# Retention two units to a burst, their kv in the banks of hp, beside a two-layer feed-forward on one Trainium2 core

## The chip, the cores and the metric

The kernel runs on one core of a Trainium2 chip. The metric is the device time of one execution in microseconds. Three runs of the kernel before took 873.88, 873.92 and 877.14 us; their median is 873.92 us.

## The reference

Linear attention with decay (retention), then two feed-forward layers without residuals:

```python
for t in range(S):                       # q, k, v: (4, 8, 768, 64)
    state = gamma[None, :, None, None] * state + np.einsum('bhd,bhe->bhde', k[:, :, t], v[:, :, t])
    y[:, :, t] = scale * np.einsum('bhd,bhde->bhe', q[:, :, t], state)
x = y.transpose(0, 2, 1, 3).reshape(3072, 512)
h = x @ w_in1                            # 512 x 2048
x = np.where(h > 0, h, np.exp(np.minimum(h, 0)) - 1) @ w_out1     # 2048 x 512
h = x @ w_in2                            # 512 x 1024
e = np.exp(h - h.max(-1, keepdims=True))
solu = h * e / (e.sum(-1, keepdims=True) + 1e-9)
ln = (solu - solu.mean(-1, keepdims=True)) / np.sqrt(solu.var(-1, keepdims=True) + 1e-6) * g_ln
out = ln @ w_out2                        # 1024 x 512
```

## The kernel before

**Precision.** Each product of the two layers is made of three matmuls on a high and a low part of both operands (`mm3`, lines 70 to 72), so that one product of 128x128 by 128x512 is three large matmuls.

**Retention in units.** A unit is 64 positions of one batch row with all eight heads; there are 48 (NU), in blocks of 8 (UPB). Four batch rows take turns, so the state that unit u leaves is used by unit u + 4. Per unit, TensorE makes scores (line 199), kv, the product of k and v that goes into the next state (line 206), and the values: state times q (line 246) and masked scores times v (line 249), all as 64x64 matmuls in a quarter of the array. The trace counts 16 instructions for the scores, 16 for kv, 16 for state times q and 16 for scores times v. VectorE reads the results from the two PSUM banks of the tile `ab`: `pt`, the masked scores (line 210), the output into `xf` (line 254) and the new state (line 223); ScalarE copies half of the state to the other partitions (line 226); GpSimd multiplies the state by its decay (line 233) and k by its factors (line 190); SP loads a unit's 576 KB (line 185) into one of three buffers.

**First layer in steps.** A block of 512 tokens (xf, split by `split_xh` on ScalarE and `split_xl` on VectorE into a high and a low part) goes through 16 steps, one for each 128 of the 2048 hidden columns; there are 6 blocks and 96 steps. Step s = 16 tb + k does `ff1_in(s)`, 12 large matmuls into `hp`, one of two PSUM banks (pool psh); the activation (`elu_a`: exp on ScalarE, line 304; `elu_b`: VectorE, lines 313 and 314, the last read of hp, then the cast gh on ScalarE, line 315, and gl on GpSimd, line 323); and `ff1_out(s - 2)`, 12 large matmuls into the four banks of `acc`. With the two of `ab` the eight PSUM banks are taken. At a block's last step the four banks of acc are copied out and stored.

**The order is written by hand.** Every engine takes its instructions in program order. The first block's retention runs ahead of step 0. From then on a unit's retention stands in a burst between `ff1_in(s)` and `ff1_out(s - 2)` of every odd step from 1 to 77, and of step 14: scores and kv of unit u + 1, then the values of unit u. The state of one burst is read in the next, so each engine has two steps for its part. At the last step of a block (k = 15) the next block's x is split: in the first block ahead of the activation, in the next four behind exp, with `elu_b` between the two splits. The split overwrites the x that `ff1_in` of that step reads, so it starts when these matmuls are over; `ff1_in` of the next step reads it.

**Second layer in 24 tiles** of 128 tokens. For tile i: `ff2_in(i)` (24 large matmuls into two banks), `norm_a(i)` (maximum, exp, product and sum; then the centering of z on GpSimd, line 394), `turn` and `turned` (a 32x32 transpose on VectorE, line 414, a store to DRAM and four loads back), `split_zh` on ScalarE and `split_zl` on VectorE, `norm_b`, and `ff2_out(i)` two tiles later (24 large matmuls, first reader of zh and zl). `split_y(i + 2)` casts the input of a later tile (line 366), when its load has landed.

Of the kernel before, what the change touches and what calls it, by code (L numbers as in the profile page):

```python
# [9 lines left out]
F32 = mybir.dt.float32  # L10
# [5 lines left out]
AF = mybir.ActivationFunctionType  # L16
ALU = mybir.AluOpType
# [4 lines left out]
P = 128  # L22
B, H, S, D = 4, 8, 768, 64
# [4 lines left out]
C = 64  # L28
NCH = S // C
# [6 lines left out]
NU = B * NCH  # L36
UPB = TB // C
LAG = 2
HL = NF1 - 1
SG = 2  # L40
HALF_N = 232
# [3 lines left out]
def tile_retention_ffn(ctx, tc, qkv, w_in1, w_out1, w_in2, w_out2, g_ln, dmask, odec, kgdec, ident_in, out):  # L45
# [28 lines left out]
    with tc.manual_schedule():  # L74
# [105 lines left out]
        blk = lambda t, p, base, n: t[half(p), base + n * D:base + (n + 1) * D]  # L180

        def load_unit(u):
            pool, n = (first_p, 4) if u < 4 or u == UPB - 1 else (at_p, 3)
            t = pool.tile([P, 18 * D], F32, tag="in", name="in", bufs=n)
            nc.sync.dma_start(out=t, in_=qkv[u])
            in_t[u] = t
# [5 lines left out]
        chunk = lambda u: u // UPB * (UPB // B) + u % UPB // B  # L192
        place = lambda u: u % B * (UPB // B) + u % UPB // B

        def att_scores(u, banks):
            t = in_t[u]
            for j, a, m in heads(lambda x, y, z: (y, z, x)):
                n = 2 * (a != j) + m
                nc.tensor.matmul(banks[j][half(a), m * C:(m + 1) * C], blk(t, j, K, n), blk(t, j, Q, n), start=True, stop=True)  # L199

        def att_kv(u, banks):
            t = in_t[u]
            if chunk(u) < NCH - 1:
                for j, a, m in heads(lambda x, y, z: (z, y, x)):
                    n = 2 * (a != j) + m
                    nc.tensor.matmul(banks[a][half(j), 4 * C + m * D:4 * C + (m + 1) * D], blk(t, a, KR, n), blk(t, a, V, n), start=True, stop=True)  # L206

        def att_mask(u, v):
            pt = at_p.tile([P, 2, 2 * C], F32, tag="pt", name="pt")
# [22 lines left out]
                four = lambda t: t.rearrange("p a (m d) -> p (a m) d", m=2)  # L232
                nc.gpsimd.tensor_tensor(four(sg_t[u]), four(s_t[u][0]), kg_sb[:, 1].unsqueeze(2).to_broadcast([P, 4, D]), ALU.mult)

        def att_values(u, banks):
            c = chunk(u)
            t, pt = in_t.pop(u), p_t.pop(u)
            col = lambda o: slice(2 * C + o * C, 2 * C + (o + 1) * C)
# [12 lines left out]
        def att_done(u, v):  # L251
            ci = place(u)
            four = lambda t: t.rearrange("p (a o) t -> p a o t", a=2)
            nc.vector.tensor_tensor(four(xf[:, :, ci * C:(ci + 1) * C]), v[:, :, 2 * C:4 * C].rearrange("p a (o t) -> p a o t", o=2), four(od_sb), ALU.mult)

        x_t = {}

# [121 lines left out]
        def norm_a(i):  # L379
            hp = h2.pop(i)  # L380
            st = sm_p.tile([P, 8], F32, tag="st", name="st")
            if i == 0:
                e, z = xf[:, :2], xf[:, 2:]
            else:
                e = z_p.tile([P, 2, 512], F32, tag="e2", name="e2")
                z = z_p.tile([P, 2, 512], F32, tag="z", name="z")
            nc.vector.tensor_reduce(st[:, 0:1], hp, AX.XY, ALU.max, negate=True)
            nc.scalar.activation(e, hp, AF.Exp, bias=st[:, 0:1], accum_out=st[:, 1:2])
            nc.vector.tensor_scalar(st[:, 2:3], st[:, 1:2], 1e-9, None, ALU.add)
            nc.vector.reciprocal(st[:, 3:4], st[:, 2:3])  # L390
            nc.vector.scalar_tensor_tensor(z, hp, st[:, 3:4], e, ALU.mult, ALU.mult, accum_out=st[:, 4:5])
            nc.vector.tensor_scalar(st[:, 5:6], st[:, 4:5], -1.0 / FF2, None, ALU.mult)  # L392
            if i < N2 - 1:
                nc.gpsimd.tensor_scalar(z, z, st[:, 5:6], 1.0, ALU.add, ALU.mult)  # L394
            else:
                t = z_p.tile([P, NF2, 4, 32], F32, tag="t", name="t")
                nc.gpsimd.tensor_scalar(t.rearrange("p c a f -> p a c f"), z.rearrange("p n (a c f) -> p (n a) c f", a=2, c=NF2), st[:, 5:6], 1.0, ALU.add, ALU.mult)
                z = t.rearrange("p c a f -> p (c a f)")
            zc_t[i] = (z, e if i else spare(), st)
# [119 lines left out]


        NS = NB * NF1
        for s in range(NS + LAG):
            tb, k = divmod(s, NF1)
            u = UPB + s // 2 + (s > NF1 - 2) if s % 2 else (2 * UPB - 1 if s == NF1 - 2 else NU)
            if s < NS:
                ff1_in(s)
                if k == NF1 - 1 and tb == 0:
                    split_xh(1, range(KD))
                    split_xl(1, range(KD))
                elu_a(s, tb == 0)  # L530
                if k == NF1 - 1 and 0 < tb < NB - 1:
                    split_xh(tb + 1, range(KD))
                    elu_b(s, tb == 0)
                    split_xl(tb + 1, range(KD))
            if u < NU:
                if u + 1 < NU:
# [3 lines left out]
                if u + 1 < NU:  # L540
                    att_mask(u + 1, both[1])
                att_done(u, both[1])
                if u + 1 < NU:
                    att_state(u + 1, both[1])
                if u + 2 < NU:
                    att_decay(u + 2)
                if u + 3 < NU:
                    load_unit(u + 3)
                if u + 2 < NU:
                    scale_k(u + 2)  # L550
            if tb == 0:
                prep_w(order1, slot)
                slot += 1
            if s < NS and (k < NF1 - 1 or tb in (0, NB - 1)):
                elu_b(s, tb == 0)
            if s == NS + LAG - 2:
                ff2_in(0)
                norm_a(0)
                turn(0)
                turned(0)  # L560
                norm_b(0)
                split_y(2)
            if s >= LAG:
                ff1_out(s - LAG)
            if tb == 0:
                prep_w(order1, slot)
                slot += 1
                elu_c(s, nc.vector)
            if s == HL:
                for i in range(slot, len(order1) + 2):  # L570
                    prep_w(order1, i)
                slot = len(order1) + 2
                ph0.close()
                ph0 = ExitStack()
                yt_p = ph0.enter_context(tc.tile_pool(name="yt0", bufs=3, side="right", reuse_waits="tile"))
            if u == NU - 1:
                ph0.close()
                right.close()
                pha.close()
                right = ExitStack()  # L580
                psr = right.enter_context(tc.tile_pool(name="psr", bufs=1, space=PSUM, side="right", reuse_waits="tile"))
                stage_p = right.enter_context(tc.tile_pool(name="stage2", bufs=5, side="right", reuse_waits="tile"))
                yi_p = right.enter_context(tc.tile_pool(name="yi", bufs=3, side="right", reuse_waits="tile"))
                yt_p = right.enter_context(tc.tile_pool(name="yt", bufs=3, side="right", reuse_waits="tile"))
                ys_p = right.enter_context(tc.tile_pool(name="ys", bufs=2, side="right", reuse_waits="tile"))
                new_top()
                nc.sync.dma_start(out=ident, in_=ident_in)
                nc.sync.dma_start(out=g_sb, in_=g_ln)
                for i in range(-4, 0):
                    prep_w(order2, i)  # L590
            if tb == NB - 1:
                prep_w(order2, k)
                if k in (1, 2, 3):
                    load_y(k - 1)
                if k in (9, 11):
                    split_y((k - 9) // 2)
            if tb == NB:
                prep_w(order2, NF1 + k)
# [4 lines left out]
        for i in range(1, N2):  # L603
# [4 lines left out]
            split_zh(i - 1)  # L608
            if i == 1:
                split_zl(0)  # L610
            if i + 2 < N2:
                split_y(i + 2)
            if i < N2 - 1:
                turn(i)
                turned(i)
            if i > 1:
# [79 lines left out]
```

## Time and profile before

| | |
|---|---|
| median of three runs | 873.92 us |
| the profiled execution | 874.49 us |
| its span, first to last instruction | 872.70 us |
| TensorE busy | 857.3 us (98%) |
| VectorE / ScalarE / GpSimd busy | 438.7 / 330.6 / 322.8 us |

The profile is of one execution. Its views have one row for an instruction or for a group of like ones: line of the kernel, engine, operation, output and inputs by name, shape; times in microseconds from the start of the span, durations in us or, where marked so, in ns. PE is TensorE, DVE VectorE, ACT ScalarE, POOL GpSimd, SPq the queue that issues the transfers. In the timeline a matmul's duration includes its way through the array, so the distance between two starts, not the duration, is what a matmul costs. In the chain the pieces follow each other from end to end.

### The profile page before, as it was taken

The numbers are of one execution on the slowest core, as the hardware profiler recorded it, in microseconds if no ns is written. First come the engines' busy times: TensorE is split into PE (matmuls) and PEld (weight loads), VectorE is DVE, ScalarE is ACT, GpSimd is POOL, SyncE is SP. The second block draws the span as 40 slices with busy tenths as digits, with TensorE's granted clock in tenths as the row PEclk, the third lists the DMA queues.
The fourth block names the chain that finished last, engine by engine and source line by source line (L and its number), as shares of the span: only waits on it lengthen the run. The fifth ranks groups of instructions, "written<-read, shape, count | busy, mean of one in ns | idle before, by whom it ended". The sixth has DMA issues, their size and how long they took to land.

```text
span 872.7 us, 15630 instructions
## 1 busy us (share of the span) xinstructions
PE 857.3 (98%) x6432; PEld 702.8 (81%) x6432; DVE 438.7 (50%) x736; ACT 330.6 (38%) x575; POOL 322.8 (37%) x321
## 2 busy tenths in 40 slices
PE   6899999999999999999999999999999999999998
PEld 5788888888888888888888878888788888888887
DVE  4899983222522233222422268796555555555552
ACT  3677762222322233222321245443343333333333
POOL 4555533322323232332322245553443333333330
PEclk9999999999999999999999999999999999999999
DMA  8677623111311113110311116310644444444432
GB/s 331 229 232 236 206 98 104 56 46 37 103 56 55 36 48 104 56 55 29 102 56 31 55 67 205 97 48 1 200 150 145 145 146 145 145 145 145 145 122 71
DMA packets 59735, 97.81 MB, mean 112 GB/s; under 512 B 4880, under 2 KB 41360, under 8 KB 59664
## 3 DMA queue, kind: packets, MB, share of 16 engines
q1 hardware_dynamic: 59664, 96.82, 34.0%
q8 instruction: 50, 0.82, 0.4%
q14 instruction: 21, 0.17, 0.1%
HBM read 72.16 MB, written 24.64 MB: 111 GB/s over the span
## 4 chain that ended last, share of the span: by engine, by line
PE 91%; DMA 3%; DVE 3%; ACT 1%; issue 1%; SPq 0%; POOL 0%; ACTq 0%; DVEq 0%
PE hp L71 14%; PE hp L72 14%; PE hp L70 14%; PE acc L70 11%; PE acc L72 10%; PE acc L71 10%; PE op L72 4%; PE op L70 4%; PE op L71 4%; PE ab L199 2%; DMA in<-in_qkv 2%; PE ab L206 1%; PE ab L246 1%; PE ab L249 1%; DMA zt<-t_dr 1%; DMA t_dr<-t 1%
## 5 line engine op out<-in xcount | busy, mean ns | idle before, releaser
L323 POOL TENSOR_TENSOR gl<-e,gh 128x512 fp32r<-128x512 f32 x80 | 106.9, 1336 | 310.9 <-issue 158.1
L70 PE MATMUL acc<-gh,w1oh 128*128 128x512 f32 x384 | 153.9, 401 | 0.4 <-ACT w1oh L138 0.4
L72 PE MATMUL acc<-gh,w1ol 128*128 128x512 f32 x384 | 150.0, 391 | 0.2 <-DVE w1ol L146 0.2
L71 PE MATMUL acc<-gl,w1oh 128*128 128x512 f32 x384 | 149.8, 390 | 0.0
L71 PE MATMUL hp<-xl,w1ih 128*128 128x512 f32 x380 | 147.9, 389 | 0.4 <-DVE xl L267 0.4
L70 PE MATMUL hp<-xh,w1ih 128*128 128x512 f32 x380 | 147.9, 389 | 0.0
L72 PE MATMUL hp<-xh,w1il 128*128 128x512 f32 x380 | 147.8, 389 | 0.0
L304 ACT ACTIVATE e<-hp 128x512 f32<-128x512 f32 x80 | 47.8, 597 | 186.0 <-PE hp L72 186.0
L313 DVE TENSOR_SCALAR e<-e 128x512 f32<-128x512 f32 x80 | 38.5, 481 | 136.3 <-ACT e L304 136.1
L315 ACT CAST gh<-e 128x512 fp32r<-128x512 f32 x96 | 59.6, 621 | 95.1 <-DVE e L314 82.7
L70 PEld LDWEIGHTS acc<-gh,w1oh 128*128 128x128 f32 x384 | 72.0, 188 | 17.1 <-ACT w1oh L138 0.8
L72 PEld LDWEIGHTS acc<-gh,w1ol 128*128 128x128 f32 x384 | 72.1, 188 | 15.9 <-DVE w1ol L146 0.6
L210 DVE TENSOR_TENSOR pt<-ab,dm_sb 128x256 f32<-128x256 f32 x43 | 18.1, 421 | 131.1 <-PE ab L249 124.6
L71 PEld LDWEIGHTS hp<-xl,w1ih 128*128 128x128 f32 x380 | 71.3, 188 | 15.7 <-DVE xl L267 0.9
L71 PEld LDWEIGHTS acc<-gl,w1oh 128*128 128x128 f32 x384 | 72.1, 188 | 14.0
L72 PEld LDWEIGHTS hp<-xh,w1il 128*128 128x128 f32 x380 | 71.3, 188 | 14.8
L70 PEld LDWEIGHTS hp<-xh,w1ih 128*128 128x128 f32 x380 | 71.3, 188 | 14.8
L117 POOL MEMSET raw<- 128x512 uint16 x48 | 61.0, 1279 | 48.7 <-DVE w1il L146 18.2
L394 POOL TENSOR_SCALAR z<-z,st 128x1024 f32<-128x1024 f32 x22 | 27.8, 1263 | 138.2 <-DVE st L392 138.2
L72 PE MATMUL op<-w2oh,zl 128*128 128x512 f32 (+1 forms) x192 | 74.2, 386 | 1.4 <-DVE zl L435 1.4
L70 PE MATMUL hp<-w2ih,yh 128*128 128x512 f32 x192 | 74.7, 389 | 0.0
L71 PE MATMUL hp<-w2il,yh 128*128 128x512 f32 x192 | 74.7, 389 | 0.0
(118 smaller groups left out, 1411.7 us busy)
## 6 DMA issues: line engine op xcount, KB each, us to landing
in<-in_qkv SPq DMA_DIRECT2D x48, 576.0 KB, 4.2
raw<-in_w_in SPq DMA_DIRECT2D x24, 512.0 KB, 3.8
raw<-in_w_out SPq DMA_DIRECT2D x24, 512.0 KB, 4.1
t_dr<-t SPq DMA_DIRECT2D x22, 512.0 KB, 2.8
zt<-t_dr SPq DMA_DIRECT2D x88, 128.0 KB, 2.5
y_dr<-yt SPq DMA_DIRECT2D x24, 256.0 KB, 2.7
yin<-y_dr SPq DMA_DIRECT2D x24, 256.0 KB, 3.4
out<-ot SPq DMA_DIRECT2D x23, 256.0 KB, 2.8
```

The costliest lines, as they stand in the source:

```text
L70: nc.tensor.matmul(o, lh, rh, start=first, stop=False)
L71: nc.tensor.matmul(o, lh, rl, start=False, stop=False)
L72: nc.tensor.matmul(o, ll, rh, start=False, stop=last)
L117: nc.gpsimd.memset(quarter(x, 3, U16), 0)
L199: nc.tensor.matmul(banks[j][half(a), m * C:(m + 1) * C], blk(t, j, K, n), blk(t, j, Q, n), start=True, stop=True)
L206: nc.tensor.matmul(banks[a][half(j), 4 * C + m * D:4 * C + (m + 1) * D], blk(t, a, KR, n), blk(t, a, V, n), start=True, stop=True)
L210: nc.vector.tensor_tensor(pt, v[:, :, :2 * C], dm_sb, ALU.mult)
L304: nc.scalar.activation(e, h_t[s], AF.Exp)
L313: nc.vector.tensor_scalar(e, e, 1.0, -1.0, ALU.min, ALU.add)
L315: nc.scalar.copy(gh, e)
L323: engine.tensor_tensor(gl, e, gh.bitcast(F32), ALU.subtract)
L394: nc.gpsimd.tensor_scalar(z, z, st[:, 5:6], 1.0, ALU.add, ALU.mult)
```

## The change

From unit 16 on (blocks 3 to 6) the retention goes in pairs of units, (16, 17), (18, 19), and so on to (46, 47). A burst `pair_burst(p)` makes the values of pair p and the scores and kv of pair p + 1. Scores take columns 0 to 255 of each bank of `ab`, values columns 256 to 511, and the kv goes into two tiles of the pool psh, which are the two banks that hp uses. The burst stands at steps 17, 20, 23, 26, 29, 33, 37, ... 77: 17 bursts. At such a step the order is `ff1_in(s)`, the activation, `ff1_out(s - 2)`, the burst, `ff1_out(s - 1)`; the next step has no `ff1_out` of its own. VectorE masks both units' scores in one instruction, writes the outputs in two and the states in two, one for each bank. At the end of a burst GpSimd decays the states of pair p + 2 (four instructions), SP loads that pair, and GpSimd scales its k. Units 8 to 15 keep their bursts; step 14 has only the values of unit 15, and step 15 none. Units 18 and 19 are loaded at steps 14 and 15 and again by the first pair burst.

At the last step of each of the first five blocks x is split ahead of the activation.

In the second layer, tile 1 is centered by an Identity activation with a bias on ScalarE, and its `turn` and `turned` go ahead of `split_y(3)`.

```diff
@@ load_unit @@
-            pool, n = (first_p, 4) if u < 4 or u == UPB - 1 else (at_p, 3)
+            pool, n = (first_p, 4) if u < 4 or u == UPB - 1 else (pair_p, 1) if u > U2 and u % 4 == 3 else (at_p, 3)
@@ att_scores, att_kv, att_values: the column in the bank becomes an argument @@
-        def att_scores(u, banks):
+        def att_scores(u, banks, base=0):
...
-        def att_kv(u, banks):
+        def att_kv(u, banks, base=4 * C):
...
-        def att_values(u, banks):
+        def att_values(u, banks, base=2 * C):
...
@@ new, behind att_done @@
+        pair = lambda p: (U2 + 2 * p, U2 + 2 * p + 1)
+        two = lambda t: t.rearrange("p (i c) -> p i c", i=2)
+
+        def pair_decay(p):
+            sg_t[p, "pair"] = sg = pair_p.tile([P, 2, 2, 2 * D], F32, tag="sg", name="sg", bufs=1)
+            for i, u in enumerate(pair(p)):
+                for a in range(2):
+                    nc.gpsimd.tensor_tensor(*[t.rearrange("p (m d) -> p m d", m=2) for t in (sg[:, a, i], s_t[u][0][:, a])], kg_sb[:, 1, 2 * a:2 * a + 2].unsqueeze(2).to_broadcast([P, 2, D]), ALU.mult)
+
+        def pair_burst(p):
+            back, front = (pair(p) if p >= 0 else ()), (pair(p + 1) if pair(p + 1)[0] < NU else ())
+            for i, u in enumerate(back):
+                att_values(u, both[0], 4 * C + i * 2 * C)
+            for i, u in enumerate(front):
+                att_scores(u, both[0], i * 2 * C)
+            more = front and chunk(front[0]) < NCH - 1
+            if more:
+                x = [psh.tile([P, 512], F32, tag="h", name="kv") for _ in range(2)]
+                for i, u in enumerate(front):
+                    att_kv(u, x, i * 2 * D)
+            if front:
+                pt = pair_p.tile([P, 2, 2, 2 * C], F32, tag="pt", name="pt", bufs=1)
+                nc.vector.tensor_tensor(pt, ab[:, :, :4 * C].rearrange("p a (i c) -> p a i c", i=2), dm_sb.unsqueeze(2).to_broadcast([P, 2, 2, 2 * C]), ALU.mult)
+                for i, u in enumerate(front):
+                    p_t[u] = pt[:, :, i]
+            if back:
+                ci, n = place(back[0]), place(back[1]) - place(back[0])
+                for a in range(2):
+                    xo = xf[:, 2 * a:2 * a + 2].rearrange("p o (u t) -> p o u t", t=C)[:, :, ci:ci + n + 1:n]
+                    nc.vector.tensor_tensor(xo, ab[:, a, 4 * C:].rearrange("p (i o t) -> p o i t", i=2, o=2), od_sb[:, 2 * a:2 * a + 2].unsqueeze(2).to_broadcast([P, 2, 2, C]), ALU.mult)
+            if more:
+                st = pair_p.tile([P, 2, 2, 2 * D], F32, tag="state", name="state", bufs=3)
+                sg = sg_t.pop((p + 1, "pair"))
+                for a, v in enumerate(x):
+                    nc.vector.tensor_tensor(st[:, a], sg[:, a], two(v[:, :4 * D]), ALU.add)
+                s2 = pair_p.tile([P, 2, 2 * D], F32, tag="s2", name="s2", bufs=3)
+                for j in range(2):
+                    nc.scalar.copy(s2[half(1 - j)], st[half(j), 1 - j])
+                for i, u in enumerate(front):
+                    s_t[u + B] = (st[:, :, i], s2[:, i])
+            if pair(p + 2)[0] < NU and chunk(pair(p + 2)[0]) < NCH - 1:
+                pair_decay(p + 2)
+            for u in pair(p + 2):
+                if u < NU:
+                    load_unit(u)
+            for u in pair(p + 2):
+                if u < NU:
+                    scale_k(u)
@@ norm_a @@
-            if i < N2 - 1:
+            if i == 1:
+                pass
+            elif i < N2 - 1:
                 nc.gpsimd.tensor_scalar(z, z, st[:, 5:6], 1.0, ALU.add, ALU.mult)
@@ the loop over the steps @@
+        PAIRS = {17: -1, 20: 0, 23: 1, 26: 2}
+        PAIRS.update({4 * p + 17: p for p in range(3, (NU - U2) // 2)})
         for s in range(NS + LAG):
             tb, k = divmod(s, NF1)
-            u = UPB + s // 2 + (s > NF1 - 2) if s % 2 else (2 * UPB - 1 if s == NF1 - 2 else NU)
+            u = U2 - 1 if s == NF1 - 2 else UPB + s // 2 if s % 2 and s < NF1 - 1 else U2
+            p = PAIRS.get(s)
             if s < NS:
                 ff1_in(s)
-                if k == NF1 - 1 and tb == 0:
-                    split_xh(1, range(KD))
-                    split_xl(1, range(KD))
+                if k == NF1 - 1 and tb < NB - 1:
+                    split_xh(tb + 1, range(KD))
+                    split_xl(tb + 1, range(KD))
                 elu_a(s, tb == 0)
-                if k == NF1 - 1 and 0 < tb < NB - 1:
-                    split_xh(tb + 1, range(KD))
-                    elu_b(s, tb == 0)
-                    split_xl(tb + 1, range(KD))
-            if u < NU:
+            if u < U2:
...
-                if u + 3 < NU:
-                    load_unit(u + 3)
-                if u + 2 < NU:
-                    scale_k(u + 2)
+                load_unit(u + 3)
+                scale_k(u + 2)
+            if p is not None:
+                elu_b(s, False)
+                ff1_out(s - LAG)
+                pair_burst(p)
+                ff1_out(s - LAG + 1)
...
-            if s < NS and (k < NF1 - 1 or tb in (0, NB - 1)):
+            if s < NS and p is None:
                 elu_b(s, tb == 0)
...
-            if s >= LAG:
+            if s >= LAG and p is None and s - 1 not in PAIRS:
                 ff1_out(s - LAG)
@@ at step 15, behind ph0.close() @@
+                pair_p = ph0.enter_context(tc.tile_pool(name="pair", bufs=1, side="right", reuse_waits="tile"))
                 yt_p = ph0.enter_context(tc.tile_pool(name="yt0", bufs=3, side="right", reuse_waits="tile"))
-            if u == NU - 1:
+                load_unit(U2 + 3)
+                pair_decay(0)
+            if p is not None and pair(p)[1] == NU - 1:
@@ the loop over the tiles of the second layer @@
             if i == 1:
                 split_zl(0)
+                z, _, st = zc_t[1]
+                nc.scalar.activation(z, z, AF.Identity, bias=st[:, 5:6])
+                turn(1)
+                turned(1)
             if i + 2 < N2:
                 split_y(i + 2)
-            if i < N2 - 1:
+            if 1 < i < N2 - 1:
                 turn(i)
                 turned(i)
```

## Rows read from the trace of the kernel before

**Rows 1.** The page's part 1: busy us, share of the span, instructions.

```profile
PE 857.3 (98%) x6432; PEld 702.8 (81%) x6432; DVE 438.7 (50%) x736; ACT 330.6 (38%) x575; POOL 322.8 (37%) x321
```

**Rows 2.** Busy us, 120 to 500: PE, PEld, DVE, ACT, POOL; clock; DMA.

```profile
120.00:500.00 380.00, 380.00 (x3433) 309.93 (x3424) 120.67 (x244) 105.11 (x206) 111.35 (x117) 1.00 0.19 59
```

**Rows 3.** Chain of waits in time order: start us, us, what.

```profile
204.96 0.39 PE ab L199 x16
205.35 0.23 PE ab L206 x16
...
205.82 0.23 PE ab L249 x16
206.05 0.43 PE acc L70
...
209.00 0.23 PE hp L70
...
214.44 0.23 PE hp L70
...
217.16 0.39 PE ab L199 x16
```

**Rows 4.** The same chain, two bursts without kv.

```profile
448.96 0.39 PE ab L199 x16
...
460.93 0.39 PE ab L199 x16
```

**Rows 5.** Timeline, 217 to 230 us: start, us, engine, line, operation.

```profile
222.46 0.41 DVE L210 TENSOR_TENSOR pt<-ab,dm_sb 128x256 f32<-128x256 f32 x1
...
223.53 0.39 PE L72 MATMUL hp<-xh,w1il 128*128 128x512 f32 x1
...
224.13 0.59 ACT L304 ACTIVATE e<-hp 128x512 f32<-128x512 f32 x1
...
225.21 0.69 DVE L314 TENSOR_TENSOR e<-e,hp 128x512 f32<-128x512 f32 x1
```

**Rows 6.** DMA issues: count, KB each, median us to landing.

```profile
in<-in_qkv SPq DMA_DIRECT2D x48, 576.0 KB, 4.2
```

**Rows 7.** Timeline, 508 to 516 us, ScalarE and TensorE.

```profile
509.15 2.17 ACT L262 CAST xh<-xf 128x512 fp32r<-128x512 f32 x4
...
513.16 0.39 PE L70 MATMUL hp<-xh,w1ih 128*128 128x512 f32 x1
...
514.33 0.39 PE L72 MATMUL hp<-xh,w1il 128*128 128x512 f32 x1
```

**Rows 8.** Line 267, VectorE: count, ns minimum/median/maximum.

```profile
L267 DVE TENSOR_TENSOR xl<-xf,xh x20: 680/684/1777, 121.2 to 512.2; 128x512 fp32r<-128x512 f32 x20
```

**Rows 9.** Timeline, 619 to 639 us, four engines; idle time before in brackets.

```profile
619.84 1.23 DVE L435 TENSOR_TENSOR zl<-spare,zh 128x1024 fp32r<-128x1024 f32 x1
...
619.96 2.10 POOL L394 TENSOR_SCALAR z<-z,st 128x1024 f32<-128x1024 f32 x1 [6.30 <-DVE st L392]
...
622.10 1.06 ACT L403 ACTIVATE e<-z 128x1024 f32<-128x1024 f32 x1 [2.48 <-POOL z L394]
...
622.23 0.43 DVE L366 CAST yh<-yin 128x512 fp32r<-128x512 f32 x1 [1.16 <-DMA yin<-y_dr]
...
622.57 1.24 DVE L414 STREAM_TRANSPOSE t<-z 128x1024 f32<-128x1024 f32 x1
...
631.03 1.05 ACT L429 CAST zh<-zt 128x1024 fp32r<-128x1024 f32 x1 [4.87 <-DMA zt<-t_dr]
...
631.46 0.39 PE L72 MATMUL hp<-w2ih,yl 128*128 128x512 f32 x1
...
638.52 0.39 PE L70 MATMUL hp<-w2ih,yh 128*128 128x512 f32 x1
```

**Rows 10.** Timeline, 27 to 31 us, TensorE's first large matmuls.

```profile
28.27 0.63 PE L292 MATMUL hp<-xh,w1ih 128*128 128x512 f32 x1
...
30.40 0.39 PE L292 MATMUL hp<-xh,w1il 128*128 128x512 f32 x1
```

More of the change, by code (lines that the diff above doesn't have):

```diff
@@ L38 @@
 LAG = 2
+U2 = 2 * UPB
 HL = NF1 - 1
@@ L198, in att_scores @@
                 n = 2 * (a != j) + m
-                nc.tensor.matmul(banks[j][half(a), m * C:(m + 1) * C], blk(t, j, K, n), blk(t, j, Q, n), start=True, stop=True)
-        def att_kv(u, banks):
+                nc.tensor.matmul(banks[j][half(a), base + m * C:base + (m + 1) * C], blk(t, j, K, n), blk(t, j, Q, n), start=True, stop=True)
+        def att_kv(u, banks, base=4 * C):
             t = in_t[u]
@@ L205, in att_kv @@
                     n = 2 * (a != j) + m
-                    nc.tensor.matmul(banks[a][half(j), 4 * C + m * D:4 * C + (m + 1) * D], blk(t, a, KR, n), blk(t, a, V, n), start=True, stop=True)
+                    nc.tensor.matmul(banks[a][half(j), base + m * D:base + (m + 1) * D], blk(t, a, KR, n), blk(t, a, V, n), start=True, stop=True)
         def att_mask(u, v):
@@ L233, in att_decay @@
                 nc.gpsimd.tensor_tensor(four(sg_t[u]), four(s_t[u][0]), kg_sb[:, 1].unsqueeze(2).to_broadcast([P, 4, D]), ALU.mult)
-        def att_values(u, banks):
+        def att_values(u, banks, base=2 * C):
             c = chunk(u)
             t, pt = in_t.pop(u), p_t.pop(u)
-            col = lambda o: slice(2 * C + o * C, 2 * C + (o + 1) * C)
+            col = lambda o: slice(base + o * C, base + (o + 1) * C)
             by_kind = heads(lambda x, y, z: (y if x == 0 else 1 - y, y, z))
@@ L521, in tile_retention_ffn @@
         NS = NB * NF1
+        PAIRS = {17: -1, 20: 0, 23: 1, 26: 2}
+        PAIRS.update({4 * p + 17: p for p in range(3, (NU - U2) // 2)})
         for s in range(NS + LAG):
             tb, k = divmod(s, NF1)
-            u = UPB + s // 2 + (s > NF1 - 2) if s % 2 else (2 * UPB - 1 if s == NF1 - 2 else NU)
+            u = U2 - 1 if s == NF1 - 2 else UPB + s // 2 if s % 2 and s < NF1 - 1 else U2
+            p = PAIRS.get(s)
             if s < NS:
                 ff1_in(s)
-                if k == NF1 - 1 and tb == 0:
-                    split_xh(1, range(KD))
-                    split_xl(1, range(KD))
+                if k == NF1 - 1 and tb < NB - 1:
+                    split_xh(tb + 1, range(KD))
+                    split_xl(tb + 1, range(KD))
                 elu_a(s, tb == 0)
-                if k == NF1 - 1 and 0 < tb < NB - 1:
-                    split_xh(tb + 1, range(KD))
-                    elu_b(s, tb == 0)
-                    split_xl(tb + 1, range(KD))
-            if u < NU:
-                if u + 1 < NU:
+            if u < U2:
+                if u + 1 < U2:
                     att_scores(u + 1, both[0])
@@ L539, in tile_retention_ffn @@
                 att_values(u, both[0])
-                if u + 1 < NU:
+                if u + 1 < U2:
                     att_mask(u + 1, both[1])
                 att_done(u, both[1])
-                if u + 1 < NU:
+                if u + 1 < U2:
                     att_state(u + 1, both[1])
-                if u + 2 < NU:
+                if u + 2 < U2:
                     att_decay(u + 2)
-                if u + 3 < NU:
-                    load_unit(u + 3)
-                if u + 2 < NU:
-                    scale_k(u + 2)
+                load_unit(u + 3)
[5 more added lines that the diff above has]
+                ff1_out(s - LAG + 1)
             if tb == 0:
```

## The prediction

> **What bounds the kernel now.** I read the page's busy line first: TensorE is busy 98% of the span, the next engine, VectorE, 50% [rows 1]. A busy TensorE can still be a stalled one, so I then read the busy times by stretch: from 120 to 500 us it is busy 380.00 of 380.00 us, while VectorE has 120.67, ScalarE 105.11, GpSimd 111.35 and the DMA engines 19% [rows 2]. In this stretch only fewer or cheaper TensorE instructions, or fewer switches between their kinds, can save time.
>
> The chain of waits in order of time shows what one burst costs there. The 24 large matmuls of one step take 214.44 - 209.00 = 5.44 us, 0.227 us each. Burst to burst, which is two steps and one burst, takes 217.16 - 204.96 = 12.20 us [rows 3]. So a burst of 64 small matmuls (the trace counts two instructions per matmul call) costs 12.20 - 10.88 = 1.32 us. Where the last chunk leaves out the 16 kv instructions, the period is 460.93 - 448.96 = 11.97 us [rows 4]: 16 instructions cost 0.23 us, 64 cost 0.92 to 0.94. What is left, **0.38 us, is paid once per burst**, for entering and leaving it.
>
> **The change, part by part.**
>
> *Fewer bursts.* Before, steps 14, 15, 17, ... 77 hold 33 bursts. After, step 14 keeps one (only the values of unit 15) and 17 pair bursts follow: 18. The small matmuls stay the same in number. Saved: 15 x 0.38 = **5.7 us**. The ends: if the fixed cost belonged wholly to the unit (a drain between its groups, not at the burst's edges), nothing; at most 6.0, with 0.40. I take 5.7, because the chain puts 0.16 of it into the first group (0.39 for 0.23), 0.20 into the first large matmul behind the burst (0.43 for 0.227), and takes the later groups of 16 at the bare 0.23 [rows 3].
>
> *The kv in hp's banks.* Two new waits on TensorE. First: kv may start when the activation of step s has read hp. An ordinary step: hp's last matmul starts at 223.53, exp at 224.13, the last read of hp ends at 225.21 + 0.69 = 225.90, so 2.4 us after the start of that last matmul [rows 5]. TensorE needs 2.72 us for the output matmuls put between, and then about 1.4 us for 64 value and 32 score instructions: 1.7 us spare. Second: the hp of step s+1 may start when VectorE has read the first kv bank. From the last score to there TensorE has 32 kv instructions (0.47) and 12 large matmuls (2.72), 3.2 us. VectorE in that time does pt (128x512 now; nearest is the 0.69 of the same shape reading hp), two outputs and one state, each 0.41 like the 128x256 pt [rows 5]: 1.9 us. About 1.2 us spare. So both waits cost zero; behind the waiting matmuls stands all of TensorE's queue.
>
> *Other queues.* SP issues two loads at a burst, where it issued one every second step; units 18 and 19 are loaded twice, so 50 loads for 48. On GpSimd the scaling of k now stands behind loads that the same burst released, 4.2 us to landing (median) [rows 6], plus some for two at once. It holds up gl of step s+1, which cannot start until some 8 us after the burst's values (two times 2.72 us of matmuls, then exp, VectorE and the cast), and whose reader comes another 8 us later. The four 128x128 decays where one was 128x256 are GpSimd's too, which has 111 of 380 us busy [rows 2]. Zero, by that cover; if a landing took over 12 us, it would be gone.
>
> *Block ends.* The split of x now stands ahead of the activation at all five block ends. At the last, before, TensorE stood for xl: a matmul starts at 513.16 and the second after it at 514.33, 1.17 us for two intervals of 0.227, so 0.72 lost; the four casts took 2.17 us from 509.15 [rows 7]. One xl, 0.68 as a rule, took up to 1.78 [rows 8], while gl ran on GpSimd. After, the casts start about 0.5 us and xl about 1 us earlier and end before that step's gl starts: **0.7 us** back (ends: 0 and 0.72). At steps 31, 47 and 63 a burst no longer stands between the block's last input and the next block's first. What covers the split there is only the 2.72 us of output matmuls: the first xl (one cast 0.55, one xl 0.68, from the end of hp) is ready after about 1.5 us, the fourth after 3.5, when TensorE reaches it at 2.95 and 5.0. Zero; without that cover the 0.7 lost at the last end would be lost at each.
>
> *Tile 1 of the second layer.* TensorE's matmuls start at 631.46 and, 25 intervals later, 638.52: 7.06 us for 5.67, **1.39 us** lost, waiting for zh and zl of tile 1. Followed back: the transpose started only at 622.57, behind yh, which waited for its load until 622.23; and the centering on GpSimd took 2.10 us (from 619.96), beside VectorE's zl from 619.84 [rows 9]. After, ScalarE centers (no row shows Identity; the nearest, a 128x1024 Square, takes 1.06) until about 621.0, zl(0) ends 621.07, and the transpose, now ahead of yh, starts about 621.1: 1.45 us earlier. From its start to zh it was 631.03 - 622.57 = 8.46 us, so zh(1) starts at 629.6, ends 630.6, zl(1) ends about 631.9; the third matmul wants it at 632.15. I take 1.3 (ends: 0, and 1.39). yh(3) comes no later than before in effect: it is ready at about 622.8 against 622.66, and its matmuls start after 626.
>
> The Trainium skill, ScalarE: Activation LUTs, Table sets: the hidden batching unit, says that identity stands in every table set, so no reload comes with it; no run here shows it yet.
>
> *Sum:* 5.7 + 0.7 + 1.3 = 7.7 us. The profiled execution took 874.49 us (span 872.70): 866.8. It lies 0.57 above the median of the runs, 873.92; against that, **866.2 us**, 0.9% less. No change, for this kernel's measurement, is within 0.5% or 4.4 us: 869.6 to 878.3.
>
> **The rivals.**
>
> *Smaller gains* (the tile-1 wait only moves, its margin being 0.2 us, or the block end stays): 866.2 + 1.3 + 0.7 = 868.2 at most. Still faster. 0.17.
>
> *The fixed cost stays with the unit.* If each pair still pays 0.38 twice, or a short new wait of that size stands in each burst, only 2.0 remain: 871.9. For it: 0.16 of the cost stands with a group of small matmuls, not with the switch back. Against: only with the first group of a burst [rows 3]. 0.12.
>
> *Slower: VectorE cannot clear the banks in time.* Place: the hp of step s+1, after each of the 14 bursts that have kv. Price: one VectorE instruction beside GpSimd ran 1.78 for 0.68 [rows 8]; if all four run so, 1.9 becomes 5.0 against the 3.2 there are, 1.8 x 14 = 25 us: 891. It decides from the point where the four take over 3.2 us, and is over 878.3 when they take 4.1. Against: gl of step s is over before pt starts, and the next GpSimd work waits for these very reads. 0.05. The Trainium skill, TensorEngine Tiling (Array Packing), PSUM Bottleneck, speaks for this side: packed small matmuls speed up TensorE and not the clearing of PSUM, which may become the bound.
>
> *Slower: the pace falls.* Before its first step TensorE does only small matmuls, and the large ones right after start 0.43 us apart (five intervals from 28.27 to 30.40 [rows 10]), the pace of the 1.2 GHz level, where later ones start 0.227 apart, that of 2.4 GHz, at a granted clock of 1.00 [rows 2, 3]. If each of the 15 full bursts of 1.9 us brought this back for those five intervals: 15 x 5 x 0.2 = 15 us, 881; it decides as soon as a burst is followed by large matmuls 0.43 apart. Against: behind the bursts of before the pace is 0.227 again. 0.02. The Trainium skill, TensorE: Matmul & The Clock Gate, What's actually happening, says that the slow level is the default and activity lifts it, not what small tiles count for.
>
> **How the numbers follow.** Forecast 0.64, smaller gains 0.17, fixed cost 0.12, slower 0.07. Faster: 0.81; same: 0.12; slower: 0.07. The range runs from 864.8 (the upper ends of the terms, 8.1, and a run's 1 us) to 871.0: the first two cases and the near part of the third.
>
> **What would show it.** Right: TensorE's gaps before kv and before the hp after a burst absent; four steps and a pair burst in 4 x 5.44 + 1.88 + 0.38 = 24.0 us from burst to burst, where two periods took 24.4; 50 loads; no wait for xl at the last block end, none for zh or zl of tile 1. Wrong: a row "hp waits for state" or "kv waits for e", periods of 24.4 or more, a second table load on ScalarE.

## The result and the profile after

The changed kernel took 867.03 us in the median of four runs (866.47 to 868.61). The kernel before, run beside it, took 875.13 (873.88 to 877.14). The ratio on record is 0.9899, with a 95% interval from 0.9875 to 0.9922; the quotient of the two medians is 0.9907. So the changed kernel is 0.9 to 1.0% faster, 8.1 us by the medians. The forecast was 866.2, the range 864.8 to 871.0.

The profiled execution took 867.59 us, its span is 865.8. Busy times and loads on the page, to be held against [rows 1, 6]:

```profile
PE 851.3 (98%) x6432; PEld 702.9 (81%) x6432; DVE 443.1 (51%) x720; ACT 327.5 (38%) x548; POOL 325.7 (38%) x348
...
in<-in_qkv SPq DMA_DIRECT2D x50, 576.0 KB, 4.8
```

TensorE has the same 6432 instructions and 6.0 us less busy time; the 50 loads are as predicted. Next, the chain of waits in order of time (start us, us, what), the counterpart of [rows 3]:

```profile
229.95 0.39 PE ab L247 x16
230.34 0.23 PE ab L250 x16
...
231.04 0.47 PE ab L200 x32
231.51 0.47 PE kv L207 x32
231.97 0.43 PE acc L71
232.40 0.23 PE acc L72
...
253.96 0.39 PE ab L247 x16
```

From burst to burst it is 253.96 - 229.95 = 24.01 us, for work that took two periods of 12.20 before. The extra time stands once at the entry (0.39 for 0.23) and once in the first large matmul behind the burst (0.43 for 0.23); 32 instructions of a kind inside the burst take the bare 0.47. The list of what TensorE waited for (line waited for, total us, times, longest) is short:

```profile
PE ab L200 <- DMA in<-in_qkv: 5.2, 1, 5.2
...
PE op L71 <- ACT zh L483: 0.6, 1, 0.6
PE op L73 <- DVE zl L489: 0.5, 1, 0.5
```

It has no row in which hp or kv waits. The long load is the first of the kernel; the other two are tile 1, still there. The block end that lost 0.7 us in [rows 7] now reads so in the timeline (start us, us, engine, line, operation):

```profile
502.68 2.18 ACT L314 CAST xh<-xf 128x512 fp32r<-128x512 f32 x4 [0.23 <-PE hp L73]
...
503.33 2.91 DVE L319 TENSOR_TENSOR xl<-xf,xh 128x512 fp32r<-128x512 f32 x4 [1.54 <-ACT xh L314]
...
505.20 0.39 PE L71 MATMUL hp<-xh,w1ih 128*128 128x512 f32 x1
505.43 0.39 PE L72 MATMUL hp<-xl,w1ih 128*128 128x512 f32 x1
505.65 0.39 PE L73 MATMUL hp<-xh,w1il 128*128 128x512 f32 x1
```

The matmuls run 0.227 apart, without a gap. Tile 1 of the second layer, against [rows 9]:

```profile
613.16 1.16 ACT L672 ACTIVATE z<-z,st 128x1024 f32<-128x1024 f32 x1 [0.42 <-DVE st L444]
...
614.35 1.25 DVE L468 STREAM_TRANSPOSE t<-z 128x1024 f32<-128x1024 f32 x1
...
615.62 0.37 SPq L470 DMA_DIRECT2D t_dr<-t  x1
...
620.26 1.74 SPq L476 DMA_DIRECT2D zt<-t_dr  x4
...
624.75 1.05 ACT L483 CAST zh<-zt 128x1024 fp32r<-128x1024 f32 x1 [6.48 <-DMA zt<-t_dr]
...
625.85 0.50 PE L71 MATMUL op<-w2oh,zh 128*128 128x512 f32 x1 [0.63 <-ACT zh L483]
...
627.11 0.50 PE L73 MATMUL op<-w2oh,zl 128*128 128x512 f32 x1 [0.53 <-DVE zl L489]
```

Centering and transpose came early, as planned. But the loads of zt were issued 4.64 us after the store, where they wait for it to land (2.84 us before). TensorE lost more here than before, not less.

**Where the time went.** I take three stretches from the starts of the matmuls: from the first matmul into acc to `ff2_in(0)` (the first layer); from `ff2_in(3)` to `ff2_in(4)`, which holds the output of tile 1 and is 48 intervals or 10.88 us without a wait; and from `ff2_in(23)` to the end of the span, 26.85 in the kernels that do not wait there. Worked out from the traces, in us:

| kernel | span | first layer | tile 1 | last tile to end |
|---|---|---|---|---|
| before | 872.7 | 560.07 | 12.28 | 27.47 |
| after | 865.8 | 553.52 | 12.62 | 26.85 |
| e1, pairs alone | 872.2 | 558.00 | 12.57 | 27.92 |
| e2, no pairs | 870.9 | 559.33 | 10.96 | 28.61 |
| e3, two bursts | 872.2 | 559.32 | 12.96 | 26.83 |
| e4, old block end | 869.6 | 558.00 | 10.93 | 26.85 |
| e5, shifted | 866.0 | 553.56 | 10.95 | 27.91 |
| e6, tile 1 late | 863.3 | 553.56 | (moved) | 26.85 |
| e7, one mask more | 865.6 | 553.49 | 11.15 | 26.86 |
| e8, four masks more | 889.2 | 576.05 | 11.29 | 27.86 |
| r1, after again | 864.7 | 553.29 | 11.25 | 28.73 |
| r2, after again | 865.1 | 553.55 | 10.91 | 26.85 |
| r3, before again | 874.0 | 560.06 | 12.56 | 27.48 |
| r4, e6 again | 863.6 | 553.50 | (moved) | 26.84 |

Of the 6.9 us between the two spans, 6.55 come from the first layer, 0.62 from the end, 0.1 from the head (what lies ahead of the first matmul into acc) and small stretches, and tile 1 takes 0.34 back. The first layer repeats to 0.3 us between executions of the same kernel; tile 1 and the end do not. The experiments had to explain both.

### The profile page after: what moved, and what is told of

Same layout as the page of the kernel before. It is cut to its first block, busy times and chain, and to the rows that moved or that the text cites. A ratio compares the mean times of both kernels' runs of the same rounds, so it can differ in the third digit from the quotient of the medians.

```text
span 865.8 us, 15617 instructions
## 1 busy us (share of the span) xinstructions
PE 851.3 (98%) x6432; PEld 702.9 (81%) x6432; DVE 443.1 (51%) x720; ACT 327.5 (38%) x548; POOL 325.7 (38%) x348
## 4 chain that ended last, share of the span: by engine, by line
PE 94%; DMA 3%; DVE 2%; ACT 1%; issue 0%; SPq 0%; DVEq 0%; ACTq 0%
PE hp L73 14%; PE hp L71 14%; PE hp L72 14%; PE acc L71 11%; PE acc L73 10%; PE acc L72 10%; PE op L73 5%; PE op L72 5%; PE op L71 5%; DMA in<-in_qkv 2%; PE ab L247 1%; PE ab L200 1%; PE ab L250 1%; PE kv L207 1%; DMA t_dr<-t 1%; PE hp L344 1%
## 5 line engine op out<-in xcount | busy, mean ns | idle before, releaser
L365 DVE TENSOR_SCALAR e<-e 128x512 f32<-128x512 f32 x80 | 46.7, 584 | 218.1 <-ACT e L356 217.9
L448 POOL TENSOR_SCALAR z<-z,st 128x1024 f32<-128x1024 f32 x21 | 25.6, 1219 | 130.9 <-DVE st L444 130.9
L71 PE MATMUL op<-w2oh,zh 128*128 128x512 f32 (+1 forms) x192 | 74.1, 386 | 0.6 <-ACT zh L483 0.6
```

Source lines behind the costliest of these rows:

```text
L71: nc.tensor.matmul(o, lh, rh, start=first, stop=False)
L365: nc.vector.tensor_scalar(e, e, 1.0, -1.0, ALU.min, ALU.add)
```

## The experiments

The kernel before took 875.97 us in the median beside e1 to e4, 876.53 beside e5 to e8 and 875.05 beside r1 to r4. Line numbers in an experiment can stand some lines off those of the changed kernel.

**e1, the pairs alone.** The changed kernel with the old block ends and the old tile 1:

```diff
-                if k == NF1 - 1 and tb < NB - 1:
+                if k == NF1 - 1 and tb == 0:
...
+                if k == NF1 - 1 and 0 < tb < NB - 1:
+                    split_xh(tb + 1, range(KD))
+                    elu_b(s, tb == 0)
+                    split_xl(tb + 1, range(KD))
...
-                z, _, st = zc_t[1]
-                nc.scalar.activation(z, z, AF.Identity, bias=st[:, 5:6])
-                turn(1)
-                turned(1)
```

> The pair bursts alone; block ends and tile 1 in the order of before. Theory (0.38 us is paid per burst, and a split of x behind the activation costs TensorE 0.72 us wherever no burst stands between): 15 bursts saved give 5.8 us; at steps 31, 47 and 63 the wait for xl that stood only at step 79 appears, three times 0.72. So 3.6 us less than before, ratio 0.996, and four waits of TensorE for xl in the profile. Rival (the 2.72 us of output matmuls cover the split in either order, and step 79 is special): 5.8 us less, ratio 0.993, one such wait. Rival (the cost stays with the unit): no gain beyond 0.3%.

Measured: 872.47 us, ratio 0.9968 (0.9954 to 0.9982). The first layer took 558.00: of 6.55 us, 2.07 are left, where 3.6 were expected. In the list of TensorE's waits, the wait for xl, which the list of before has once (0.4 us), now stands four times:

```profile
PE hp L72 <- DVE xl L319: 2.2, 4, 0.6
```

So the pairs save 5.8 us of fixed cost only together with the new block ends; alone they give 3.8 of it back there, and not the 2.2 of three ends at 0.72. e4 shows why.

**e2, the block ends and tile 1 without the pairs.** The kernel before with those two parts of the diff, its retention untouched.

> The other two parts alone; the bursts stay single. Theory: 0.7 us from the last block end, and at tile 1 between a gain of 1.3 (the store to DRAM lands in 2.8 us) and a loss of 0.4 (it lands in 4.6, as in the profile of the changed kernel): ratio 0.997 to 1.000, by whether an instruction packet falls into the store. Rival (tile 1 is slowed by ScalarE's centering or by the order itself): zh late by over 0.5 us with a store of 2.8 us.

Measured: 872.58 us, 0.997 (0.9956 to 0.9983). The first layer took 559.33, 0.74 less than before: the one end, as predicted (0.72). Tile 1 took 10.96, a loss of 0.08 where before lost 1.40: the term of 1.3 can be had. In the queue's rows of the timeline the zt loads follow 2.93 us behind the store:

```profile
620.70 0.37 SPq L418 DMA_DIRECT2D t_dr<-t  x1
623.63 2.08 SPq L424 DMA_DIRECT2D zt<-t_dr  x4
```

But the end took 1.14 us more than in the kernel before: zh and zl of tile 22 came late, behind a load of zt that landed 5.2 us after its issue (3.45 in the kernel before).

**e3, the pair burst cut in two.** The values ahead of `ff1_out(s - 2)`, scores and kv behind it; 15 more bursts, the same small matmuls:

```diff
 def pair_burst(p):
-            for i, u in enumerate(back):
-                att_values(u, both[0], 4 * C + i * 2 * C)
...
 the loop over the steps
             if p is not None:
+                for i, u in enumerate(pair(p) if p >= 0 else ()):
+                    att_values(u, both[0], 4 * C + i * 2 * C)
                 elu_b(s, False)
                 ff1_out(s - LAG)
                 pair_burst(p)
```

> The changed kernel, but the values of the pair stand ahead of the output matmuls of step s - 2 and scores and kv behind them, so that a pair burst is cut into two with the same instructions. Theory (a fixed cost per burst): 15 more bursts cost 15 x 0.38 = 5.7 us over the changed kernel: ratio 0.996 to 0.997 to before; from burst to burst 24.4 us where the changed kernel has 24.0. Rival (the cost goes with units or groups, or the gain came from the place of the bursts): as the changed kernel, 0.990, and 24.0.

Measured: 872.23 us, 0.9969 (0.9957 to 0.998). The first layer took 559.32, 5.80 more than after: 0.387 for each added burst. The chain shows both halves paying at either end:

```profile
229.05 0.39 PE ab L247 x16
229.44 0.23 PE ab L250 x16
...
230.14 0.43 PE acc L71
...
233.09 0.62 PE ab L200 x32
233.71 0.47 PE kv L207 x32
234.18 0.43 PE acc L71
...
253.45 0.39 PE ab L247 x16
```

The scores now carry the entry (0.62 for 0.47), a second 0.43 stands behind the values, and the period is 24.40 again. The fixed cost belongs to the burst, not to the unit. The Trainium skill, TensorEngine Tiling (Array Packing), Key Properties, says that a change of the tiling mode drains TensorE. These rows fit that, and give the price here, 0.39 for going in and coming out; the drain itself no row shows.

**e4, the old block ends in the changed kernel** (the first two hunks of e1's diff).

> The changed kernel with the split of x behind the activation, as before. Theory: four waits of TensorE for xl, 0.72 each, 2.9 us over the changed kernel: ratio 0.993 to before. Rival (only step 79 waits): 0.7 over it, ratio 0.991.

Measured: 870.8 us, 0.9942 (0.9922 to 0.9962). The first layer took 558.00, so 4.48 more than after: 1.12 at each of four ends, not 0.72. The timeline of one of them:

```profile
217.42 1.30 POOL L375 TENSOR_TENSOR gl<-e,gh 128x512 fp32r<-128x512 f32 x1 [2.56 <-ACT gh L367]
...
218.19 0.81 DVE L365 TENSOR_SCALAR e<-e 128x512 f32<-128x512 f32 x1 [1.57 <-ACT e L356]
...
219.64 3.59 DVE L319 TENSOR_TENSOR xl<-xf,xh 128x512 fp32r<-128x512 f32 x4
...
220.02 0.39 PE L71 MATMUL hp<-xh,w1ih 128*128 128x512 f32 x1
...
220.38 0.50 PE L72 MATMUL hp<-xl,w1ih 128*128 128x512 f32 x1
...
220.72 0.40 PE L73 MATMUL hp<-xh,w1il 128*128 128x512 f32 x1
...
220.88 1.80 POOL L375 TENSOR_TENSOR gl<-e,gh 128x512 fp32r<-128x512 f32 x1 [2.16 <-ACT gh L367]
...
222.35 0.40 PE L71 MATMUL hp<-xh,w1ih 128*128 128x512 f32 x1
...
223.28 0.50 PE L72 MATMUL hp<-xl,w1ih 128*128 128x512 f32 x1 [0.54 <-DVE xl L319]
```

There are two gaps: at the first xl (0.36 for 0.227) and at the fourth (0.93), and after each the next matmul starts 0.34 instead of 0.227 later. The other three ends have the same two gaps, 0.36 and 0.93 to 0.94. The first gap is new. The step ahead of the block end has no output matmuls any more, so its gl on GpSimd runs beside VectorE's first instruction of the last step, which takes 0.81 for its usual 0.43, and what follows on VectorE starts late. (This is read from the rows; no run takes that overlap away alone.) The second gap is the old one: this step's gl (220.88) lies beside the four xl, 3.59 us for them where the changed kernel's take 2.91. The Trainium skill, SBUF — State Buffer, Who interferes with whom, says that the two engines share a pair of SBUF ports, which an instruction of one can hold to its end while the other waits; the stretched rows stand beside GpSimd's in each case shown here.

**e5, a shift.** To see whether the late landing hangs on when the store is issued, six score matmuls of unit 0 are made twice ahead of the first layer:

```diff
-        def att_scores(u, banks, base=0):
+        def att_scores(u, banks, base=0, only=8):
...
         att_scores(0, sets[0][0])
+        att_scores(0, sets[0][0], only=6)
```

> The changed kernel with six of the score matmuls of unit 0 made a second time at the very start, where TensorE waits for data: 24 more TensorE instructions ahead of everything, the results the same. Theory (the wait at tile 1 in the profile came from a packet of 16 KB of TensorE's instructions that went through the same DMA engine as part of the store): the packet is asked for 24 instructions, or 2.7 us, earlier, lands ahead of the store, the store takes 2.8 us and the two large gaps at tile 1 (1.7 us lost) shrink under 0.4. Rival (the store is slow because it now follows the loads of the next tiles, or by its earlier place): it takes over 4 us again, 1.7 lost.

Measured: 868.33 us, 0.9904 (0.9889 to 0.9919). Tile 1 took 10.95, a loss of 0.07, and its store landed in 3.0 us, much as the theory had it; but the end took 1.06 more than after, so nothing was gained. What the shift did can't be told from what another execution would have shown anyway; r1 and r2 were run for that.

**e6, the output of tile 1 behind the input of tile 4.** 

```diff
             ff2_in(i)
+            if i == 4:
+                ff2_out(1)
...
-            if i >= 2:
+            if i >= 2 and i != 3:
                 ff2_out(i - 2)
```

> The changed kernel with the second product of tile 1 behind the first product of tile 4 instead of ahead of it, 5.4 us later; tile 2's follows at once. Theory (TensorE waits only for zh and zl of tile 1, whatever made them late): no gap at tile 1, also with a slow store; 1.7 us less than the changed kernel in a profile with the slow store, 0.1 to 0.4 less where the store is quick: ratio 0.988 to 0.990 to before. Rival (the wait only moves, to the second product of tile 2, now reached without that pause): 0.990, and a gap of over 0.5 us there.

Measured: 865.79 us, 0.9873 (0.9852 to 0.9895). From `ff2_in(3)` to `ff2_in(5)` it took 21.76 us, 96 bare intervals; after took 23.50. TensorE does not wait there, since zh and zl of tile 1 now have 5.44 us more. But the store landed in 2.85 us in this profile (2.84 in r4), and with such a store the changed kernel itself took 21.79 (r2): that the wait stays away behind a slow store is not shown.

**e7 and e8, VectorE's spare time.** The masking of the scores is repeated once, or four times, in the 14 bursts that have kv:

```diff
             if more:
+                for _ in range(4):
+                    nc.vector.tensor_tensor(pt, ab[:, :, :4 * C].rearrange("p a (i c) -> p a i c", i=2), dm_sb.unsqueeze(2).to_broadcast([P, 2, 2, 2 * C]), ALU.mult)
```

> The changed kernel with the masking of the scores made twice in each of the 14 bursts that have kv, about 0.6 to 0.7 us more on VectorE ahead of the reads of the kv banks. Theory (about 1.2 us spare): no change, ratio 0.990, no wait of hp for the state. Rival (no spare): 0.7 x 14 = 10 us more, ratio 1.00.

Measured for one: 866.91 us, 0.9883 (0.9866 to 0.9901); the first layer 553.49, as in after.

> The same with the masking made five times, 2.5 to 2.8 us more. Theory (1.2 us spare): 1.3 to 1.6 us in each of 14 bursts, 18 to 22 us: ratio 1.011 to 1.016, and a wait of TensorE at the first matmul of hp behind each burst. Rival (the hp of the next step does not wait for these reads): 0.990.

Measured for four: 890.92 us, 1.0161 (1.0146 to 1.0176). TensorE's list of waits gets the row that the forecast named as the sign of the slower rival, and the timeline shows it at one burst:

```profile
PE hp L71 <- DVE state L296: 18.2, 14, 1.4
```

```profile
241.75 2.87 DVE L286 TENSOR_TENSOR pt<-ab,dm_sb 128x512 f32<-128x512 f32 x4
...
243.99 0.39 PE L73 MATMUL acc<-gh,w1ol 128*128 128x512 f32 x1
...
244.53 0.74 DVE L291 TENSOR_TENSOR xf<-ab,od_sb 128x256 f32<-128x256 f32 x2
245.20 0.74 DVE L296 TENSOR_TENSOR state<-sg,kv 128x256 f32<-128x256 f32 x2
...
245.66 0.50 PE L71 MATMUL hp<-xh,w1ih 128*128 128x512 f32 x1 [1.29 <-DVE state L296]
```

The four cost 244.53 - 241.75 = 2.78 us on VectorE and 1.67 - 0.23 = 1.44 in the gap at hp, so some 1.3 us had been spare. Over 14 bursts the first layer took 22.5 us more than after, 1.61 each; 1.55 of it is the gap shown and the slow restart behind it (0.34 for 0.23).

**r1 to r4, the same kernels again.** Does the landing at tile 1 belong to the program or to the execution? The changed kernel twice more, the kernel before once more, and e6 once more for a comparison in one session.

> The changed kernel itself, with nothing edited, to see whether tile 1's loss belongs to the program or to the execution. Theory (the landing of the store of tile 1 varies from execution to execution): the store lands in 2.8 to 3.2 us here instead of 4.6, and ff2_in(3) to ff2_in(4) takes 10.9 to 11.3 us instead of 12.62; the span is then about 864.1 to 864.4 instead of 865.8. Rival (the delay is fixed by the place of the instruction in the program): again 4.6 us and 12.6 us. From the first output matmul to ff2_in(0) both expect 553.5 us. The ratio to the kernel before: 0.988 to 0.991.

> The changed kernel a third time, one look. Theory (varies by execution): the landing and the loss differ again from the other looks, between 2.8 and 4.8 us and 0 to 2.1 us. Rival (fixed by the program): 4.6 us and 1.74 us in each.

> The kernel before, with nothing edited, a second look at its tile 1 and at its last tiles. At tile 1 the store is late by the centering in any execution, so the loss should be at least 1.3 us again (ff2_in(3) to ff2_in(4) 12.2 us or more; more if the store lands late). At tile 22 the theory (the wait there is a landing that varies by execution) lets the 1.0 us of the first look be anything from 0 to 2 us; the rival (fixed by the program) expects 1.0 us again.

> The version with the output of tile 1 behind the input of tile 4, again, in the same session as the changed kernel, to compare the two. Theory (a wait at tile 1 of 0 to 2 us in the changed kernel, by execution, and none here): 0.5 to 1.5 us less than the changed kernel by medians, ratio to the kernel before 0.987 to 0.989. Rival (nothing gained in the mean): the medians of the two agree within 0.4 us.

Measured: the same program gave 12.62, 11.25 and 10.91 us at tile 1 in three executions. From issue to landing the stores of line 470 took, at the least, in the median and at the most, first in after, then in r1:

```profile
DMA to landing us min/median/max: 2.8/2.8/4.6
```

```profile
DMA to landing us min/median/max: 2.8/2.8/2.8
```

So the 4.6 us do not come with the program each time: r1 and r2 had 2.84 and 2.85. With nearly equal stores these two still lost 0.37 and 0.03, so r2's forecast, that landing and loss would differ again, holds for the loss alone. The 4.6 is not unique either: in e3, another first layer with the same tile 1, the store took 4.8. The kernel before lost again (12.56), with a store of 2.8.

At the end the changed kernel took 26.85, 28.73 and 26.85; the kernel before 27.47 and 27.48. So the end varies in the changed kernel; in the kernel before it was the same twice, as the rival of r3 had it. What varies is the landing of the four zt loads of tile 22, first in after, then in r1:

```profile
843.47 1.74 SPq L476 DMA_DIRECT2D zt<-t_dr  x4
...
847.40 1.05 ACT L483 CAST zh<-zt 128x1024 fp32r<-128x1024 f32 x1 [0.34 <-DMA zt<-t_dr]
```

```profile
840.48 1.74 SPq L476 DMA_DIRECT2D zt<-t_dr  x4
...
846.82 1.04 ACT L483 CAST zh<-zt 128x1024 fp32r<-128x1024 f32 x1 [2.75 <-DMA zt<-t_dr]
```

From their issue to zh it is 3.93 us in after and 6.34 in r1, whose last load took 4.9 to land.

By medians r1 took 866.02 us (five runs; 0.9882 to 0.9917 of before) and r4 866.07 (0.9895, 0.9879 to 0.9912). The expected 0.5 to 1.5 us for e6 did not come out: the rival holds, in line with the 0.03 and 0.37 that the changed kernel lost at tile 1 in that session's two profiles, and no version tried is shown to be faster than the changed kernel.

## Why the prediction was right, and where it was not

The forecast of 7.7 us for the profiled execution stands against 6.9 there, and 867.03 lies 0.8 above the 866.2, inside the range; the same kernel's other session had 866.02. That the end figure came so near is in part luck. The forecast stood on a median of 873.92, and the kernel before took 875.13 beside the changed one, so the base was 1.2 us too low and the gain by medians 8.1. In the profiled pair, tile 1 fell 1.6 us short of its term, while the end gave 0.6 that no term had. Taken from the first output matmul on, so without the head, the means of two profiles of before and three of after lie 7.4 us apart.

The rival of smaller gains was right about tile 1 in the profiled execution and wrong about the block end. The median lies between its 868.2 and the forecast, and only the stretches tell the two apart.

*Fewer bursts: right.* 5.7 predicted. The first layer gave 6.55; less the 0.72 of the block end that is 5.83, and e3, which puts 15 bursts back, takes 5.80. The reading from [rows 3, 4], 0.38 once per burst, held to 0.01 us, and with it the rival of a cost that stays with the unit falls.

*The kv in hp's banks: right in its waits, a little cautious in its spare.* For the second wait I had 1.9 us of VectorE against 3.2 of TensorE. Beside a burst the timeline of the changed kernel has:

```profile
231.57 0.69 DVE L281 TENSOR_TENSOR pt<-ab,dm_sb 128x512 f32<-128x512 f32 x1
232.18 0.75 DVE L288 TENSOR_TENSOR xf<-ab,od_sb 128x256 f32<-128x256 f32 x2
232.84 0.74 DVE L293 TENSOR_TENSOR state<-sg,kv 128x256 f32<-128x256 f32 x2
...
234.76 0.39 PE L71 MATMUL hp<-xh,w1ih 128*128 128x512 f32 x1
```

The first state ends near 232.84 + 0.41 = 233.25, 1.5 us ahead of hp (1.2 predicted); e8 finds 1.3 at its burst. At the first wait VectorE's last read of hp ended at 229.11 in the same burst and the first kv matmul started at 231.33, 2.2 us later (1.7 predicted). The place and the kind of price of the slower rival were right: e8 ends at 891, by four instructions more than there are. The limit that the Trainium skill, TensorEngine Tiling (Array Packing), PSUM Bottleneck, names is one which no burst of the changed kernel reaches.

*Other queues: right.* 50 loads, 4.8 us to landing; no wait of TensorE follows from them.

*Block ends: 0.72 right, its cover mis-priced.* The step "without that cover the 0.7 lost at the last end would be lost at each" had the right sign and a wrong size: e4 pays 1.12 at each of four ends, because the pairs also move the activations of the last two steps together. The step failed where I carried the 0.72 of [rows 7] over to a kernel whose order around the block end had changed. So the new block ends are worth 4.5 us to the changed kernel, not 0.7; the sum did not suffer, since pairs and new block ends came together.

*Tile 1: wrong in the profiled execution, right in others.* The step "from its start to zh it was 631.03 - 622.57 = 8.46 us" carried a duration over in which two transfers lie. In after it was 624.75 - 614.35 = 10.40: the transpose came early as worked out, and the store took the gain and 0.34 more. TensorE's waits for zh and zl, whose absence was to be a sign of being right, stayed. With a store that lands in the usual time most of the term is there: 10.91 in r2, 10.96 in e2, 10.93 in e4, but 11.25 in r1. Even so the 8.46 was too short: in the nine profiles with the new order and a store of 2.8 to 3.4 us this path took 8.56 to 9.08, and the margin was 0.2. Over three executions of the changed kernel and two of before the means are 11.59 and 12.42, so 0.8 of the 1.3.

*Not in the sum: the end of the kernel*, 0.6 us in the first pair of profiles, and -1.3 with r1. The prediction has no term for it; it hangs on when the last zt loads of tile 22 land.

*The pace: right.* Behind a burst only the first large matmul takes 0.43; the granted clock over 120 to 500 us is 1.00 as in [rows 2]. One activation table load stands in the profile, as the forecast of Identity had it.

## What to carry to other kernels

When a busy engine is the bound, read from the chain what a switch between two kinds of work costs, and price the change by the number of switches: it was right to 2% here, while TensorE's busy share was 98% before and after. A change that thins out work also takes away what it covered; ask at each place where the moved work stood what now stands in its stead, since here the pairs alone gave 3.8 of 5.8 us back (e1). A path through DRAM carries its transfers' spread with it: take its time from the longest landings in the trace as well as from the median, and leave that much between the producer and the reader. One trace may not be enough: in that of before the longest store on this path took 3.1 us and the longest load 4.5, and the store of 4.6 came in another execution.

## What was not expected of the hardware

- Transfers of the same program land at different times in different executions: the 512 KB store of tile 1 in 2.8 us as a rule, 4.6 in one of three executions of the changed kernel, 4.8 in e3, and 3.0 to 3.4 in e1, e5, e7 and e8. It is not chance alone: in both profiles of the kernel before the same loads of zt land late, those of tiles 6 and 14 (4.5 and 4.5 us, 4.9 and 4.8). What holds a transfer up is open. In the trace of after, the last of the store's packets start 4.1 us after its issue, where 95% have started by 2.24, and a 16 KB packet of the queue marked "instruction" starts between them, at 2.25; but r1 and r2 have such a packet 2.5 us after the issue and no late store, and e5 has a few late packets with no such packet beside them, so the link is not shown.
- After a wait, TensorE's next matmul starts 0.34 us later instead of 0.227, at block ends and tiles alike (220.38 to 220.72 in e4): a gap costs 0.11 us more than its length. The first interval between two large matmuls behind a burst is 0.34 as well.
- The first output matmul of the first layer started between 37.4 and 40.0 us in the 14 profiles. This head, which the change does not touch, spreads wider than most of the terms argued over here. The granted clock goes with it. The last rise from 0.50 to 1.00, from the 1.2 to the 2.4 GHz level, stands at 24.9 us in r1 (start 37.4), 29.4 in e2 and e6 (38.0), 30.6 in r4 (38.3), 31.3 to 32.1 in e1, e4, e5, e8 and r2 (39.5 to 39.9), 32.7 in e7 (40.0) and 33.0 in r3 (39.9); ahead of it TensorE had small matmuls with waits between them, and large ones that fell there ran 0.43 us apart. In before, after and e3 the record of the clock starts only at 30.4 to 30.8 us. No run was made to part the clock from the wait for data.
